# The second MLP matmul as seven half-size products (Strassen's identity) instead of eight, in a fused attention and MLP kernel

## The chip, the cores and the metric

One core of a Trainium2 chip runs the kernel. The time is the device time of one execution in microseconds (us); the kernel before took 689.41 us (median of 3 runs, 689.25 to 690.89). The engines are PE (TensorE, matmuls; PEld is its weight loading), DVE (VectorE), ACT (ScalarE), POOL (GpSimd), and SP, whose queue issues most of the DMAs. Each engine works through its own instructions in program order and waits on semaphores for the others.

## The reference

The input `x` is 2048 tokens by 512. The output mixes two branches by a gate per token:

```python
x = A_x
g = _sigmoid((x * gate_w).sum(-1, keepdims=True))
a = _A_ref(x, A_wqkv, A_wo)                 # 32 heads of 16, causal window of 256, then @ wo
b = _B_ref(x, B_w1, B_b1, B_w2, B_b2)       # gelu(layernorm(x) @ w1 + b1) @ w2 + b2
return g * a + (1 - g) * b
```

The change touches the last product of `_B_ref`, `h @ w2`: `h` is 2048 tokens by 1792 (the hidden width F), `w2` is 1792 by 512. All of it is float32.

## The kernel before, in words

A float32 product is made of three matmuls on `float32r` operands: every operand is split into a high part (a rounded copy, by ACT's `copy` or a DVE cast) and a low part (`lo_part`, line 132: the value minus its high part, a DVE subtraction with two operands in SBUF), and high x high, high x low and low x high are summed in PSUM.

The program runs in stages. Up to about 110 us the projections for q, k and v are made. Up to about 480 us attention runs, with the first MLP matmul (line 651) filled in between; its results, before the activation, go to DRAM as `hp`, a block of 128 hidden rows by 512 tokens for each of 4 token chunks and 14 hidden blocks. The last stage, from 487 us on, is the one that the change rewrites. It is one loop over 56 items (chunk c, hidden block f). For each item PE runs 12 matmuls (line 881, `mlp2`): 4 blocks of 128 tokens by three high/low pairs; the stationary operand is 128x128 of `h`, the moving one is a 128x512 part of `w2`. Four PSUM banks collect a chunk over its 14 items.

What feeds the loop is written out by hand in program order. `load_h` brings a block of `hp` six items ahead, ACT applies the GELU (line 707) two items ahead, DVE makes the high part (cast, line 711) and the low part (line 133) one item ahead. In chunk 0 the blocks of `w2` are split as well (ACT copy, DVE subtraction).

Into the same loop goes the attention's output projection, `attn_out`, once for each chunk and for 4 blocks b of 128 tokens. `scale(b)` multiplies the attention's sum by the reciprocal of its denominator (DVE, line 839) and splits the product (ACT copy, DVE subtraction). `mm(b)` runs 12 matmuls with `wo` (line 850), then ACT scales the result by the gate (line 857) and DVE adds the bias share (line 858; chunk 0 is finished on line 853 instead). `after(n, f)` queues `f` for n items later. The four `scale(b)` are queued when `attn_out` is called, each `mm(b)` when its `scale(b)` runs; so at one item `scale(b + 1)` stands ahead of `mm(b)`. Two PSUM banks (`o0`, `o1`) take the `mm` in turn.

At a chunk's last item, line 895 adds the four MLP sums, times the gate, into the output block `us` and stores it (chunk 0: lines 889 and 890). The functions around the change, in the numbering of the profile:

Of the kernel before, what the change touches and what calls it, by code (L numbers as in the profile page):

```python
# [19 lines left out]
S = 2048  # L20
# [6 lines left out]
FT = F // 128  # L27
C = 512
# [33 lines left out]
def gated_mix_kernel(ctx, tc: tile.TileContext, xt, x2, wq0, wqk, wv, wo, xa, gw, w1, w2, b1, b2, out):  # L62
# [608 lines left out]
    w2s, wos, w2t, spare = {}, {}, [], []  # L671

    def load_w2(f):
        if f % 2 == 0:
            w2t.append(x8())
            if f == 2:
                spare.append(x8())
        w = w2s[f] = w2t[-1][:, f % 2 * 2 * C:f % 2 * 2 * C + 2 * C].rearrange("p (k n) -> p k n", k=2)
        raw = t2()
        sp.dma_start(raw, w2[f])  # L680
        return lambda both=False: split(w, raw, both)
# [7 lines left out]
    def early_w2():  # L689
        for n in range(6):  # L690
            def go(n=n):
                fn = load_w2(n)
                after(2, lambda: fn(True))
            after(1 + n, go)
# [5 lines left out]
    hs = {}  # L700

    def load_h(c, f):
        s = t2()
        sp.dma_start(s, hp[c, f])

        def gelu():
            act.activation(s, s, AF.Gelu_apprx_tanh, bias=b1s[:, f:f + 1])  # L707

        def parts(dst=None):
            h, l = dst or (t2(F32R), t2(F32R))  # L710
            dve.tensor_copy(h, s)  # L711
            lo_part(l, s, h)
            hs[c, f] = h, l

        return gelu, parts
# [10 lines left out]
    def block(p, kb):  # L726
# [10 lines left out]
        if p == 7 and kb == 12:  # L737
            early.extend(load_h(0, f) for f in range(2))
# [39 lines left out]
    for f, (gelu, _) in enumerate(early):  # L778
        gelu()
# [16 lines left out]
    nt[0] = 28  # L796
    waiting = {}
    for f in range(2, 4):
        waiting[0, f] = load_h(0, f)
    for f in range(4, 6):  # L800
        waiting[0, f] = load_h(0, f)
# [3 lines left out]
    for f in range(2, 4):  # L805
        waiting[0, f][0]()
        waiting[0, f] = (lambda: None), waiting[0, f][1]
    low, high = {"o0": 1, "o1": 1, "a4": 1, "a5": 1}, {f"a{i}": 1 for i in range(4)}
    open_psum(*((low, high) if "b0" in used else (high, low)))
    b2s = get("work", "b2s", 1, (128, D))  # L810

    after(1, gate)
    after(4, lambda: early_wo(2, 4))
    after(7, lambda: sp.dma_start(b2s, view(b2, [0, 128], [1, D])))
    us = {}

    def attn_out(c):
# [154 lines left out]
```

## Time and profile before

| | |
|---|---|
| median of 3 runs | 689.41 us |
| the profiled execution, its own time | 689.64 us |
| its span (first to last instruction) | 687.8 us |
| PE busy over the span | 681.1 us (99%) |
| last stage, 487.0 to 683.8 us: PE / DVE / ACT / POOL busy | 196.64 / 108.55 / 62.73 / 0.00 us |
| mean granted TensorE clock | 0.999 |

The span is what the trace covers; 1.8 us of the execution's time lie outside it. Busy times overlap between engines. An instruction's duration includes a run-out that the next one on the same engine may overlap, so that the distance from start to start is shorter than the duration. "128x512" in a row means 128 partitions by 512 elements in each.

### The profile page before, as it was taken

How to read it: one execution, taken by the hardware profiler on the slowest of the kernel's cores; microseconds unless marked ns; L12 is line 12 of the kernel's file. 1: busy time of each engine (PE TensorE's matmuls, PEld its weight loads, DVE VectorE, ACT ScalarE, POOL GpSimd, SP SyncE). 2: the span in 40 equal slices, each digit the busy share in tenths (PEclk: the TensorE clock that was granted, in tenths of full speed). 3: DMA queues.
4: the chain of work that ended last, by engine and by line, in shares of the span. 5: the costliest groups of instructions: out<-in, count | busy, mean ns of one | idle time of the engine just before them, and what ended most of it. 6: DMA issues, size and time to landing. Idle time of an engine off the chain costs nothing.

```text
span 687.8 us, 15593 instructions
## 1 busy us (share of the span) xinstructions
PE 681.1 (99%) x5674; PEld 535.5 (78%) x5674; DVE 476.4 (69%) x970; ACT 384.6 (56%) x637; POOL 265.9 (39%) x622
## 2 busy tenths in 40 slices
PE   9999999999999999999999999999999999999997
PEld 6887777877768777877787777777787888888886
DVE  6737789968777787777686877855575545556454
ACT  6438453457677776877758777687633224123231
POOL 6800156426666664765656566568000000000000
PEclk9999999999999999999999999999999999999999
DMA  8998888786575767566676555527876450841801
GB/s 322 354 290 266 278 262 267 217 253 224 176 211 173 247 211 228 174 214 188 190 240 207 168 185 153 178 96 240 288 238 204 143 173 5 275 126 41 253 1 62
DMA packets 89620, 137.91 MB, mean 200 GB/s; under 512 B 13160, under 2 KB 36648, under 8 KB 89416
## 3 DMA queue, kind: packets, MB, share of 16 engines
q1 hardware_dynamic: 81384, 128.72, 59.1%
q10 hardware_dynamic: 8160, 8.19, 3.9%
q8 instruction: 45, 0.74, 0.4%
q14 instruction: 31, 0.25, 0.1%
HBM read 81.53 MB, written 54.30 MB: 197 GB/s over the span
## 4 chain that ended last, share of the span: by engine, by line
PE 96%; ACT 1%; DVE 1%; DMA 1%; issue 0%; POOL 0%; SPq 0%; DVEq 0%; ACTq 0%
PE ps_b L651 22%; PE ps_a L881 22%; PE ps_b L441 13%; PE ps_d L308 12%; PE ps_b L418 7%; PE ps_b L362 7%; PE ps_d L338 7%; PE ps_o L850 6%; PE ps_d L295 1%; PE ps_x L362 1%; DMA qk<-qk 1%; PE ps_x L279 1%; ACT x L420 0%; DVE us L895 0%; DVE us L889 0%; ACT pb L420 0%
## 5 line engine op out<-in xcount | busy, mean ns | idle before, releaser
L651 PE MATMUL ps_b<-x,w 64*128 64x512 f32 x1344 | 207.1, 393 | 0.0
L881 PE MATMUL ps_a<-x,t 128*128 128x512 f32 x648 | 150.2, 389 | 0.2 <-DVE t L711 0.2
L372 DVE TENSOR_REDUCE mx<-ps_b 128x2 f32<-128x512 f32 x208 | 144.1, 693 | 7.1
L881 PEld LDWEIGHTS ps_a<-x,t 128*128 128x128 f32 x648 | 121.5, 188 | 26.2 <-DVE t L711 0.6
L651 PEld LDWEIGHTS ps_b<-x,w 64*128 64x128 f32 x1344 | 127.4, 186 | 10.5 <-ACT x L136 0.3
L371 DVE COPY_PREDICATED ps_b<-tri,ps_b 128x256 f32<-128x256 uint8 x208 | 88.4, 425 | 52.7 <-PE ps_b L362 40.6
L422 POOL TENSOR_SCALAR_AFFINE_SELECT pa<-pa 128x256 f32<-128x256 f32 x192 | 74.2, 414 | 57.7 <-ACT pa L420 56.7
L420 ACT ACTIVATE pa<-ps_b 128x768 f32<-128x768 f32 x96 | 76.5, 813 | 24.7 <-PE ps_b L418 13.3
L418 PE MATMUL ps_b<-qk 50*128 50x384 f32 (+5 forms) x512 | 87.8, 339 | 0.1
L308 PE MATMUL ps_d<-x,w 128*128 128x512 f32 x360 | 84.7, 390 | 0.0
L362 PE MATMUL ps_b<-qk 62*128 62x384 f32 (+3 forms) x472 | 83.0, 345 | 1.0 <-DMA qk<-qk 0.8
L308 PEld LDWEIGHTS ps_d<-x,w 128*128 128x128 f32 x360 | 67.3, 188 | 14.5 <-issue 0.5
L420 ACT ACTIVATE pb<-ps_b 128x768 f32<-128x768 f32 (+2 forms) x96 | 66.2, 706 | 20.5 <-PE ps_b L418 9.7
L422 POOL TENSOR_SCALAR_AFFINE_SELECT pb<-pb 128x256 f32<-128x256 f32 x160 | 62.2, 415 | 37.4 <-ACT pb L420 36.9
L707 ACT ACTIVATE t<-t,b1s 128x512 f32<-128x512 f32 x56 | 38.6, 716 | 44.0 <-DMA t<-hp 43.6
L418 PEld LDWEIGHTS ps_b<-qk 50*128 50x128 f32 (+1 forms) x512 | 48.8, 184 | 16.0 <-issue 3.2
L422 POOL TENSOR_SCALAR_AFFINE_SELECT x<-x 128x256 f32<-128x256 f32 x128 | 49.3, 414 | 29.7 <-ACT x L420 29.3
L420 ACT ACTIVATE x<-ps_b 128x768 f32<-128x768 f32 x64 | 50.7, 813 | 14.0 <-PE ps_b L418 9.7
L362 PEld LDWEIGHTS ps_b<-qk 62*128 62x128 f32 (+1 forms) x472 | 45.1, 184 | 17.2 <-issue 3.9
L338 PE MATMUL ps_d<-wv,x 128*128 128x512 f32 x192 | 46.7, 394 | 0.0
L850 PE MATMUL ps_o<-w,t 128*128 128x512 f32 x192 | 46.1, 389 | 0.0
L441 PE MATMUL ps_b<-pa,v 128*32 128x128 f32 (+2 forms) x704 | 42.9, 345 | 0.3 <-ACT x L420 0.2
(96 smaller groups left out, 757.1 us busy)
## 6 DMA issues: line engine op xcount, KB each, us to landing
qk<-qk SPq DMA_DIRECT2D x112, 196.0 KB
t<-hp SPq DMA_DIRECT2D x56, 256.0 KB
hp<-t SPq DMA_DIRECT2D x54, 256.0 KB
qk<-t SPq DMA_DIRECT2D x48, 256.0 KB
osc<-x SPq DMA_DIRECT2D x31, 256.0 KB
t<-in_w SPq DMA_DIRECT2D x28, 256.0 KB
w<-w SPq DMA_DIRECT2D x28, 256.0 KB
qk<-t ACTq DMA_DIRECT2D x24, 256.0 KB
```

Of the source, the lines that this page charges most:

```text
L308: pe.matmul(o, a[:, dt * 128:(dt + 1) * 128], b[:, dt * C:(dt + 1) * C], start=n == 0, stop=n == 11)
L338: pe.matmul(o, x[:, a:a + 128], wvs[dt][:, k], start=n == 0, stop=n == 11)
L362: pe.matmul(o[:, e, :n], qs[pr][r:k, qb * 128:qb * 128 + 128], ks[pr][r:k, t0:t0 + n], start=True, stop=True)
L371: dve.copy_predicated(o[:, :, :128], tri, o[:, :, 256:384])
L372: dve.tensor_reduce(m, o[:, :, :256], mybir.AxisListType.X, ALU.max)
L418: pe.matmul(o[:, e, :w], ks[pr][r:k, kb * 128:kb * 128 + 128], qs[pr][r:k, kb * 128:kb * 128 + w], start=True, stop=True)
L420: act.activation(pt[:, :, :w], o[:, :, :w], AF.Exp, scale=0.25)
L422: pool.affine_select(out=pt[:, :, a:a + 128], in_=pt[:, :, a:a + 128], pattern=[[0, 2], [sgn, 128]], base=b, channel_multiplier=-sgn, comp ...
L441: pe.matmul(a[32 * h:32 * h + 32, at:at + w], vs[:, kb, v:v + 32], pts[p, kb][:, h, fr:fr + w], start=n == 0, stop=n == len(parts) - 1, sk ...
L651: pe.matmul(o[:, e], w[kt // 4][r:r + 64, k, m:m + 128], y[r:r + 64, a:a + C], start=n == 0, stop=n == 23)
L850: pe.matmul(a, x[:, g], wos[g][:, k], start=n == 0, stop=n == 11)
L881: pe.matmul(accs[c][b], x[:, b * 128:(b + 1) * 128], w, start=f == 0 and n == 0, stop=f == FT - 1 and n == 2)
```

## The change

Strassen's identity multiplies two 2x2 block matrices with seven block products instead of eight. Here a token chunk is halved (256 + 256 tokens), the hidden axis is halved (block i and block i + 7 go together), and the 512 outputs are halved (256 + 256). One step s is such a pair of hidden blocks in one chunk: 7 steps in each chunk, 28 in all. In each step, `product(s, k)` for k = 0 to 6 runs 6 matmuls (line 1013 of the changed kernel): 2 blocks of 128 tokens by three high/low pairs, now with a 128x256 moving operand. Seven PSUM banks, one for each k, collect a chunk.

The operands of the seven products are sums and differences of the quarters of `h` (5 of them, and 2 quarters as they are) and of `w2` (again 5 and 2). Per step, POOL makes the 5 sums of `h`, and for steps 1 to 6 POOL makes 3 and DVE 2 of the sums of `w2` (`sums`, line 696 by way of `mix`). Each of the 7 operands is then split: ACT copies 256 + 256 + 1280 columns, DVE subtracts the same (line 134). Casts on DVE are gone from this stage. `w2`'s operands are made in chunk 0 and kept. `h` has two sets of operands in turn. Step 0 is prepared in the attention stage.

At the last step of a chunk, `spread(c, k)` adds each product, times plus or minus the gate, into the one or two output quarters that contain it: 24 DVE instructions of 128x256 (line 1021) where there were four of 128x512. In the last chunk the last two steps run interleaved, product by product. `attn_out` is now placed by a table of (step, product) places; `mm` has one PSUM bank.

```diff
+NP = FT // 2
...
+    def part(pair, x, a, b):
+        low, high = (f(a, b) for f in pair)
+        copy(high, x)
+        lo_part(low, x, high)
+
+    def pairs_of(a, b):
+        a, b = (room(t) for t in (a, b))
+        return a(0, 1), a(1, 2), b(0, 1), b(1, 2)
+
+    def mix(to, x, y, op, eng):
+        eng.tensor_tensor(out=to, in0=x, in1=y, op=op)
+
+    def sums_w(raw, ab, ks, eng, n=0):
+        a0, a1, b0, b1 = ab
+        sums = ((a1, b1, ALU.subtract), (a0, b0, ALU.subtract), (a0, a1, ALU.add), (b0, b1, ALU.add), (a0, b1, ALU.add))
+        for k in ks:
+            mix(raw(k - n, k - n + 1), *sums[k], eng)
+
+    def sums_h(raw, ab, ks, eng, n=0):
+        a0, a1, b0, b1 = ab
+        sums = {2: (a1, a0, ALU.subtract), 3: (b1, b0, ALU.subtract), 4: (a0, b1, ALU.add),
+                5: (a0, b0, ALU.add), 6: (a1, b1, ALU.add)}
+        for k in ks:
+            mix(raw(k - n, k - n + 1), *sums[k], eng)
...
-    t = spare[0]
-    rooms = [(t[:, f * 2 * C:f * 2 * C + C], t[:, f * 2 * C + C:f * 2 * C + 2 * C]) for f in range(2)]
-    for f in range(2):
-        early[f][1](rooms[f])
+    hs = {0: [room(x8()[:, :NP * 256]) for _ in range(2)]}
+    ab = pairs_of(*early)
+    part(hs[0], ab[0], 0, 1)
+    part(hs[0], ab[3], 1, 2)
+    for ks in ((2, 3), (4,), (5, 6)):
+        raw = room(t2())
+        sums_h(raw, ab, ks, dve if ks[0] < 5 else pool, ks[0])
+        part(hs[0], raw(0, len(ks)), ks[0], ks[-1] + 1)
...
+    def raw_w(i):
+        tag = (None, "ra", "us0", "us1", "high6", "us1", "us1")[i]
+        t = get("work", tag, 1, *(((128, NP * 256),) if tag == "high6" else ((128, 4, 512),)))
+        if tag != "high6":
+            t = t.rearrange("p a n -> p (a n)")
+        return room(t[:, :5 * 256])
+
+    def sums(kind, s, *engs):
+        ab = pairs_of(*raws[kind, s])
+        raw = wholes[kind, s] = raw_w(s) if kind == "w" else room(get("work", "r", 2, (128, 5 * 256)))
+        if kind == "w":
+            sums_w(raw, ab, (0, 1), engs[0])
+            sums_w(raw, ab, (2, 3, 4), engs[1])
+        else:
+            t = raws[kind, s][0]
+            sums_h(raw, ab, (2, 3, 4, 5, 6), engs[0], 2)
...
+    def parts_h(s):
+        ab, raw = pairs_of(*raws.pop(("h", s))), wholes.pop(("h", s))
+        if s == 1:
+            hs[1] = [seven(f"h{x}") for x in "lh"]
+        hs[s] = hs[s % 2]
+        part(hs[s], ab[0], 0, 1)
+        part(hs[s], ab[3], 1, 2)
+        part(hs[s], raw(0, 5), 2, 7)
+
+    def ahead(s):
+        if s < NPS:
+            gelu(s % NP, raws["h", s])
+        if s < NP:
+            sums("w", s, dve, pool)
+        if s < NPS:
+            sums("h", s, pool)
+
+    def parts(s):
+        if s < NPS:
+            parts_h(s)
+        if s < NP:
+            parts_w(s)
...
-        def scale(b, o, r):
+        def scale(b):
+            o, r = (t[x][:, :, b * 128:b * 128 + 128] for x in "or")
             dve.tensor_tensor(out=o, in0=o, in1=r, op=ALU.mult)
-            h, l = t2(F32R, (128, 4, 128)), t2(F32R, (128, 4, 128))
+            h, l = t[b] = t2(F32R, (128, 4, 128)), t2(F32R, (128, 4, 128))
             copy(h, o)
             lo_part(l, o, h)
 
-            def mm():
-                i = 4 * c + b
-                a = ps(f"o{b % 2}")
-                n = 0
-                for x, k in ((h, 0), (h, 1), (l, 0)):
-                    for g in range(NG):
-                        pe.matmul(a, x[:, g], wos[g][:, k], start=n == 0, stop=n == 11)
-                        n += 1
-                if not c:
-                    dve.scalar_tensor_tensor(out=us[c][:, b], in0=a, scalar=g0[:, i:i + 1], in1=us[c][:, b],
-                                             op0=ALU.mult, op1=ALU.add)
-                    sp.dma_start(out[i], us[c][:, b])
-                    return
-                act.activation(us[c][:, b], a, AF.Copy, scale=g0[:, i:i + 1])
-                dve.scalar_tensor_tensor(out=us[c][:, b], in0=b2s, scalar=g1[:, i:i + 1], in1=us[c][:, b],
+        def mm(b):
+            i = 4 * c + b
+            if not b:
+                us[c] = get("work", f"us{c % 2}", 1, (128, 4, 512))
+            h, l = t.pop(b)
+            a = ps("o")
+            n = 0
+            for x, k in ((h, 0), (h, 1), (l, 0)):
+                for g in range(NG):
+                    pe.matmul(a, x[:, g], wos[g][:, k], start=n == 0, stop=n == 11)
+                    n += 1
+            act.activation(us[c][:, b], a, AF.Copy, scale=g0[:, i:i + 1])
+            dve.scalar_tensor_tensor(out=us[c][:, b], in0=b2s, scalar=g1[:, i:i + 1], in1=us[c][:, b],
+                                     op0=ALU.mult, op1=ALU.add)
+
+        n = NP * c if c else 3
+        at(*((n - 6, 1) if c else (0, 2)), load_su)
+        at(*((n - 5, 1) if c else (0, 6)), inv)
+        at(*((n - 3, 5) if c else (1, 1)), load_o)
+        at(*((n - 2, 1) if c else (1, 5)), load_r)
+        for b, (p, q) in enumerate((((n - 1, 4), (n, 1)), ((n, 1), (n, 4)), ((n, 4), (n + 1, 1)), ((n + 1, 1), (n + 1, 4)))):
+            at(*p, lambda b=b: scale(b))
+            at(*q, lambda b=b: mm(b))
...
+    adds = {0: ((0, 1, 1), (1, 1, 1)), 1: ((0, 0, -1), (1, 0, -1)), 2: ((1, 1, 1),), 3: ((0, 0, -1),),
+            4: ((0, 0, 1), (1, 1, 1)), 5: ((0, 0, -1), (0, 1, 1)), 6: ((1, 0, 1), (1, 1, -1))}
+    accs = {}
+
+    def product(s, k):
+        c, i = divmod(s, NP)
+        if not i:
+            accs[k] = ps(f"a{k}")
+        (hl, hh), (wl, wh) = ([f(k, k + 1) for f in p] for p in (hs[s], w2s[i]))
+        for b in range(2):
+            for n, (x, w) in enumerate(((hh, wh), (hh, wl), (hl, wh))):
+                pe.matmul(accs[k][:, 256 * b:256 * b + 256], x[:, 0, b * 128:(b + 1) * 128], w[:, 0],
+                          start=not i and not b and not n, stop=i == NP - 1 and n == 2, skip_group_check=True)
+
+    def spread(c, k):
+        for row, col, sg in adds[k]:
+            for b in range(2):
+                i = 4 * c + 2 * row + b
+                u = us[c][:, 2 * row + b, col * 256:col * 256 + 256]
+                dve.scalar_tensor_tensor(out=u, in0=accs[k][:, 256 * b:256 * b + 256], scalar=sign[sg][:, i:i + 1], in1=u,
                                          op0=ALU.mult, op1=ALU.add)
...
+    parts(1)
+    for s in range(NPS - 2):
+        c, i = divmod(s, NP)
+        if s:
+            tick()
+            parts(s + 1)
+        ahead(s + 2)
+        if s + 3 < NPS:
+            load_raw("h", s + 3)
+        if s + 3 < NP:
+            load_raw("w", s + 3)
+        for k in range(NP):
+            for fn in plan.pop((s, k), []):
+                fn()
+            product(s, k)
+            if i == NP - 1:
+                spread(c, k)
+        if i == NP - 1:
+            for row in range(2):
+                store(c, row)
+    parts(NPS - 1)
+    c = NCH - 1
+    for k, row, cols in ((0, 0, None), (1, 0, None), (4, 0, None), (5, 0, (256, 512)), (6, 1, (0, 256)),
+                         (2, 1, (256, 512)), (3, 0, (0, 256))):
+        for s in (NPS - 2, NPS - 1):
+            product(s, k)
+        spread(c, k)
+        if cols:
+            store(c, row, slice(*cols))
+    assert not plan
```

Three places show how the instructions move. The first is DVE's queue around the output projection of chunk 1, before. L839 is `scale`'s product, the L133 after it the low part of `scale`, L858 the bias share at the end of `mm`; L711 with its L133 split a block of `h`:

```order
L839 TENSOR_TENSOR oa_7177<-oa_7177,ra_7178 128x4x128
L133 TENSOR_TENSOR t_7494<-oa_7177,t_7493 128x512
L858 SCALAR_TENSOR_TENSOR us_7216<-b2s_6889,g_86,us_7216 128x512
L711 CAST t_7514<-t_7336 128x512
L133 TENSOR_TENSOR t_7515<-t_7336,t_7514 128x512
L839 TENSOR_TENSOR oa_7177<-oa_7177,ra_7178 128x4x128
L133 TENSOR_TENSOR t_7533<-oa_7177,t_7532 128x512
L858 SCALAR_TENSOR_TENSOR us_7216<-b2s_6889,g_86,us_7216 128x512
```

The same queue of the changed kernel, at the output projection of chunk 2. L987 is the bias share, L970 `scale`'s product; the L134 with `hl` or `x_517` are the low parts of the next step's `h`:

```order
L987 SCALAR_TENSOR_TENSOR us_649_8172<-b2s_6917,g_86,us_649_8172 128x512
L970 TENSOR_TENSOR oa_7975<-oa_7975,ra_8015 128x4x128
L134 TENSOR_TENSOR t_8190<-oa_7975,t_8189 128x512
L987 SCALAR_TENSOR_TENSOR us_649_8172<-b2s_6917,g_86,us_649_8172 128x512
L970 TENSOR_TENSOR oa_7975<-oa_7975,ra_8015 128x4x128
L134 TENSOR_TENSOR t_8231<-oa_7975,t_8230 128x512
L134 TENSOR_TENSOR x_517_6824<-g_8070,x_518_6825 128x256 x2
L134 TENSOR_TENSOR x_517_6824<-r_8156,x_518_6825 128x1280
L987 SCALAR_TENSOR_TENSOR us_649_8172<-b2s_6917,g_86,us_649_8172 128x512
L970 TENSOR_TENSOR oa_7975<-oa_7975,ra_8015 128x4x128
L134 TENSOR_TENSOR t_8295<-oa_7975,t_8294 128x512
```

What moved: before, `scale` of the next block (L839) had run ahead of the bias share (L858) of the block whose matmuls were under way; the rows L839, L133, L858 belong to blocks b + 1, b + 1 and b. Now the bias share of block b (L987) stands ahead of `scale(b + 1)` (L970), since `mm(b)` and `scale(b + 1)` have the same place in the table and `mm(b)` was entered first.

The second place is the changed DVE queue at the end of chunk 1 (L1021 is `spread`; the first two rows are the low parts for the step that follows):

```order
L134 TENSOR_TENSOR x_517_6824<-g_7942,x_518_6825 128x256 x2
L134 TENSOR_TENSOR x_517_6824<-r_8000,x_518_6825 128x1280
L1021 SCALAR_TENSOR_TENSOR us_613_7627<-ps_a_612_7620,g_86,us_613_7627 128x256 x4
L1021 SCALAR_TENSOR_TENSOR us_613_7627<-ps_a_617_7648,z,us_613_7627 128x256 x4
L1021 SCALAR_TENSOR_TENSOR us_613_7627<-ps_a_618_7655,g_86,us_613_7627 128x256 x2
L1021 SCALAR_TENSOR_TENSOR us_613_7627<-ps_a_619_7662,z,us_613_7627 128x256 x2
L970 TENSOR_TENSOR oa_7975<-oa_7975,ra_8015 128x4x128
L134 TENSOR_TENSOR t_8111<-oa_7975,t_8110 128x512
L1021 SCALAR_TENSOR_TENSOR us_613_7627<-ps_a_623_7689,g_86,us_613_7627 128x256 x4
```

What moved: `scale(0)` of the next chunk now stands among the 24 `spread` instructions, and the next step's low parts stand ahead of them; before, four additions (L895) took the place of the 24.

The third place is POOL. Before, its last work was the masking of the attention probabilities; the changed queue goes on behind that (`ra`, `us` and `high` are rooms for sums of `w2`, `r` for sums of `h`):

```order
L423 AFFINE_SELECT pb_1524<-pb_1524 128x2x128 x4
L696 TENSOR_TENSOR t_6839<-t_6671,t_6672 128x256 x2
L696 TENSOR_TENSOR ra_6863<-g_6852 128x256 x3
L696 TENSOR_TENSOR r_6869<-g_6849 128x256 x5
L696 TENSOR_TENSOR us_546_6944<-g_6858 128x256 x3
L696 TENSOR_TENSOR r_6950<-g_6855 128x256 x5
```

So POOL, which had nothing in the last stage, has 8 two-operand sums for each step up to step 6 and 5 for each step after it.

More of the change, by code (lines that the diff above doesn't have):

```diff
@@ L698, in early_wo, with load_h, gelu @@
         after(k, lambda: [fn() for fn in fns])
[L700 to L715, printed above, removed]
+    def load_h(c, i, raws):
+        for k in range(2):
+            sp.dma_start(raws[k], hp[c, i + NP * k])
+    def gelu(i, raws):
+        for k in range(2):
+            f = i + NP * k
+            act.activation(raws[k], raws[k], AF.Gelu_apprx_tanh, bias=b1s[:, f:f + 1])
     cur = [None]
@@ L795, in gated_mix_kernel, with load_raw, seven @@
     open_pool("work")
[L796 to L801, printed above, removed]
+    nt[0] = 3
+    raws = {}
+    def load_raw(kind, s):
+        t = get("work", "g", 4, (128, 2, 512))
+        raws[kind, s] = [t[:, k] for k in range(2)]
+        if kind == "w":
+            load_w2(s, raws[kind, s])
+        else:
+            load_h(s // NP, s % NP, raws[kind, s])
+    def seven(tag):
+        return room(get("work", tag, 1, (128, NP * 256), F32R))
```

184 lines of the change are left out of this document (91 added, 93 removed).

## The prediction

> **What bounds the kernel now.** I read the page's busy shares first, then the engines over the last stage, then the groups of that stage.
>
> ```profile
> span 687.8 us, 15593 instructions
> PE 681.1 (99%) x5674; PEld 535.5 (78%) x5674; DVE 476.4 (69%) x970; ACT 384.6 (56%) x637; POOL 265.9 (39%) x622
> 487.00:683.80 196.80, 196.64 (x866) 161.92 (x864) 108.55 (x186) 62.73 (x98) 0.00 (x0) 1.00 0.47 149
> ```
>
> The third row is the stage that the change rewrites (columns: stretch, length, busy time of PE, PEld, DVE, ACT and POOL, granted clock, DMA). PE works 196.64 of its 196.80 us at full clock; POOL does nothing. PE's own instructions set the time here, and DVE and ACT have slack on average.
>
> ```profile
> L881 PE MATMUL ps_a<-x,t 128*128 128x512 f32 x648 | 150.2, 389 | 0.2 <-DVE t L711 0.2
> L850 PE MATMUL ps_o<-w,t 128*128 128x512 f32 x192 | 46.1, 389 | 0.0
> 545.05 2.88 PE L850 MATMUL ps_o<-w,t 128*128 128x512 f32 x12
> 547.77 2.88 PE L881 MATMUL ps_a<-x,t 128*128 128x512 f32 x12
> ```
>
> From the timeline's starts, 12 matmuls take 547.77 - 545.05 = 2.72 us: 0.227 each from start to start (389 ns is pipelined duration).
>
> **What the change saves on PE.** 28 steps of 42 matmuls with 256 columns replace 28 x 24 with 512. The trace has few of 256:
>
> ```profile
> 357.61 0.28 PE L418 MATMUL ps_b<-qk 64*128 64x256 f32 x2
> 357.73 0.40 PE L651 MATMUL ps_b<-x,w 64*128 64x512 f32 x2
> L881 PEld LDWEIGHTS ps_a<-x,t 128*128 128x128 f32 x648 | 121.5, 188 | 26.2 <-DVE t L711 0.6 <-DVE t L133 0.4
> ```
>
> After a 256-wide pair the next pair starts 0.12 us later, with new weights in both row halves. The other end is the 188 ns that a weight load lasts, if it did not overlap. I take 0.120, since that row has the very width. A step then costs 42 x 0.120 = 5.04 us on PE (a product 0.72) against 24 x 0.227 = 5.44: 28 x 0.40 = 11.2 us saved, not an eighth, because every matmul carries some 13 ns beside its columns (0.227 for 512, 0.120 for 256: the line through both leaves 0.013). The Trainium skill, TensorE: Matmul & The Clock Gate, section Back-to-back issue gap, puts a matmul at N / 2.4 + 2.5 ns; by it the step would fall from 5.2 to 4.6 us and the saving be 16 us. The trace's 227 ns against its 216 speaks for my figure.
>
> **What it adds, and its prices.**
>
> ```profile
> 9.72 4.30 DVE L133 TENSOR_TENSOR x<-v,x 128x512 fp32r<-128x512 f32 x7
> L133 DVE TENSOR_TENSOR t<-oa,t 128x512 fp32r<-128x512 f32 x16 | 11.1, 693 | 12.0 <-ACT t L136 12.0
> L858 DVE SCALAR_TENSOR_TENSOR us<-b2s,g,us 128x512 f32<-128x512 f32 x12 | 9.0, 752 | 28.1 <-ACT us L857 28.1
> L895 DVE SCALAR_TENSOR_TENSOR us<-ps_a,g,us 128x512 f32<-128x512 f32 x11 | 7.7, 751 | 3.3 <-PE ps_a L881 3.3
> L895 DVE SCALAR_TENSOR_TENSOR us<-ps_a,g,us 128x256 f32<-128x256 f32 x2 | 0.9, 480 | 0.0
> L707 ACT ACTIVATE t<-t,b1s 128x512 f32<-128x512 f32 x56 | 38.6, 716 | 44.0 <-DMA t<-hp 43.6
> L136 ACT ACTIVATE w<-wv 128x128 fp32r<-128x128 f32 x8 | 2.2, 300 | 2.4 <-DMA wv<-in_wq 2.4
> L136 ACT ACTIVATE t<-oa 128x512 fp32r<-128x512 f32 x16 | 10.1, 632 | 45.9 <-DVE oa L839 29.9 <-PE ps_a L881 10.9 <-DMA t<-hp 3.9
> L857 ACT ACTIVATE us<-ps_o,g 128x512 f32<-128x512 f32 x12 | 8.3, 690 | 29.9 <-PE ps_o L850 29.9
> L133 POOL TENSOR_TENSOR w<-t,w 128x512 fp32r<-128x512 f32 x12 | 15.5, 1292 | 5.8 <-ACT w L136 5.7
> L133 POOL TENSOR_TENSOR nm<-mx,nm 128x16 fp32r<-128x16 f32 x32 | 7.1, 222 | 2.7
> L422 POOL TENSOR_SCALAR_AFFINE_SELECT pa<-pa 128x256 f32<-128x256 f32 x192 | 74.2, 414 | 57.7 <-ACT pa L420 56.7
> ```
>
> DVE: seven subtractions in 4.30 us are 0.60 apart, 0.09 less than one lasts. The two L895 rows give 1.06 ns a column, so a two-operand instruction of 256 columns takes 0.33, of 1280 columns 1.41. The low parts of one step's `h` cost 0.33 + 0.33 + 1.41 = 2.07 us; `w2`'s as much, plus two sums, 0.66. A `spread` instruction is 0.39 (480 ns less 0.09), 24 of them 9.4 us. ACT: from 300 and 632 ns, 0.41 for 256 columns, 1.30 for 1280; a step with both splits and two GELUs is 5.7 us at full durations. POOL: no 256-wide sum is in the trace. Its ends are the one-operand 414 ns and the 512-wide 1292; the line through 222 (16 columns) and 1292 gives 0.74, 0.65 apart, and I take that, since work and operands are the same. An estimate from the Trainium skill's floor of 2.5 cycles an element at 1.2 GHz (GPSIMD Engine Reference, section 2.1) is 0.53 us; by it the result would be some 9 us lower, and the 512-wide row, 1292 against 1067, stands above it.
>
> **The shared port.** DVE and POOL do not run such work side by side:
>
> ```profile
> 100.94 0.65 DVE L133 TENSOR_TENSOR t<-ps_d,t 128x512 fp32r<-128x512 f32 x1
> 101.51 1.07 DVE L133 TENSOR_TENSOR x<-t,x 128x512 fp32r<-128x512 f32 x1
> 100.74 1.29 POOL L531 TENSOR_TENSOR t<-t,t 128x512 f32<-128x512 f32 x1
> 119.61 2.89 DVE L133 TENSOR_TENSOR x<-t,x 128x512 fp32r<-128x512 f32 x2
> 118.74 3.20 POOL L531 TENSOR_TENSOR t<-t,gws 128x512 f32<-128x512 f32 x2 [0.81 <-DMA t<-in_x]
> ```
>
> POOL's sum from 100.74 ends at 102.03. The DVE subtraction that reads PSUM runs through it in 0.65; the next, with both operands in SBUF, ends at 102.58, 0.55 after POOL. At 119 both engines pay for each other. So in the changed stage POOL's sums and DVE's low parts, `scale` and bias instructions share one resource; `spread`, which reads PSUM, does not.
>
> **Chunk 0.** A step of 1 to 6 holds that port for 8 x 0.65 (POOL) + 2.07 + 2.07 + 0.66 (DVE) = 10.0 us, twice PE's 5.04. Step 1 is prepared while PE runs step 0: begun with the stage, its pieces need 10.0 plus the last ACT copy (1.30) and DVE's 1.41, so PE waits about 12.7 - 5.0 = 7.7. Steps 1 and 2: 10.0 plus about 1 us in which the port idles while ACT copies between POOL's fifth sum and DVE's subtraction, less 5.04: 2 x 6 = 12. Steps 3 to 6 must make three more such sets (33), step 7's `h` (5 x 0.65 + 2.07 + 1 = 6.3), and four blocks of the projection with three 0.6 us instructions (7.2): 46.5 against PE's 4 x 5.04 + 4 x 2.72 = 31.0, so 15.5. Together 35 us.
>
> **The projection's order.** `mm(b)` now precedes `scale(b + 1)`. From the end of `mm(b)` to the start of `mm(b + 1)` stand PE's run-out 0.16 (389 - 227 ns), ACT 0.69, bias 0.75, product 0.69, copy 0.63, low part 0.69: 3.6 us in a row, where before the first part lay under the next `scale`. PE has three or four products in between, 2.16 or 2.88 us.
>
> **Each chunk change** (into chunks 1, 2, 3). DVE's queue from the last step's start: low parts 2.07, 24 `spread` 9.4, `scale(0)` 1.9 (0.60 + 0.63 + 0.69), the next step's low parts 2.07, bias 0.66, `scale(1)` 1.9: 18.0 us before `mm(1)`. PE has 5.04 + 0.72 + 2.72 + 2.16 = 10.6: late by 7.4. `mm(2)`: 3.6 - 2.88 = 0.7. `mm(3)`: 3.6 + 2.07 (low parts behind it) - 2.16 = 3.5. That is 11.6, plus port waits of 12 such DVE instructions, 0 to 0.65 each: 3.9 in the middle. 15.5 x 3 = 46.5 us. Behind a waiting DVE low part stand the next `spread` and `scale`; behind the waiting `mm` all later products.
>
> **The end and the clock.** Steps 26 and 27 interleave, so 27's pieces are wanted six products (4.3 us) earlier; the last `spread` adds about 1. The clock: PE has no idle gap in this stage before, but some nine of over 3 us after. At the kernel's start it shows what a cold array costs:
>
> ```profile
> 1.25 4.45 PE L279 MATMUL ps_x<-t 128*128 128x512 bf16 x10 [1.25 <-DVE t L275]
> 686.00:687.80 1.80, 0.00 (x0) 0.00 (x0) 0.00 (x0) 0.00 (x0) 0.00 (x0) 0.53 0.19 64
> ```
>
> Ten matmuls take 4.45 us where 2.27 would do, 2.2 lost, and the granted clock falls to 0.53 within four idle us at the end. Ends: 0 (the slow matmuls run while DVE is the bound) to 9 x 2.2 = 20; I take 7, one in each chunk change. The Trainium skill (TensorE: Matmul & The Clock Gate, HAM oscillation) has the clock halve after a gap of about 3.4 us, which agrees with the 0.53.
>
> **Sum.** 687.8 - 11.2 + 35 + 46.5 + 5.3 + 7 = 770.4 us of span; the profiled execution lay 1.8 above its span (689.64; the median of the runs is 689.41), so 772.
>
> **Rivals.** *The port costs nothing* (sums quick, or spread over idle moments). Chunk 0 is then bound by ACT, about 0.5 a step over PE: 3, the first step 5, its projection chains 8; chunk changes 3 x 11.6 = 35; end 5.3: 687.8 - 11.2 + 56 + 1.8 = 735 to 745. For it: on average DVE has room (108.55 of 196.8 us). Against: the two port rows. *All hidden, faster*: steps are prepared two ahead; if the prepared pieces always arrive and each chain fits under 2.16 us, only PE counts: 687.8 - 11.2 + 1 + 1.8 = 679. It decides from the point where 3.6 becomes less than 2.16, and a chunk-0 step less than 5.04; POOL's empty 196.8 us speaks for it, every price above against. *Weight loads bind* at 0.188: a step is 7.9 us, 69 more on PE, which hides part of the waits (chunk 0 12, changes 27, end 5): 687.8 + 69 + 44 + 1.8 = 803. The 0.12 row speaks against it.
>
> **Chances.** My sum 0.60 (its own range 752 to 795), port free 0.25, all hidden 0.06, weight loads 0.05, something between all hidden and port free 0.04. The range 735 to 803 leaves out the hidden cases and the tails. A difference of 0.3% (2 us) is about what runs of this kernel can tell: faster 0.07, same 0.01, slower 0.92.
>
> **What would show it.** L1013 starts 0.120 apart within a product; PE idle for 80 us or more in the stage, waiting for L134 (DVE low parts), most of it in steps 1 to 9 and behind L984 after each chunk change, and little in steps 3 to 5 of later chunks; POOL's L696 at 0.74 or more each, the 1280-wide L134 above 1.5 on the mean; the granted clock below 1 there. I am wrong if PE is busy throughout, or if the 256-wide matmuls are 0.19 apart.

## The result: 13% slower, and the profile after

The changed kernel takes 780.88 us (median of 4 runs, 779.29 to 781.02) against 689.33 us for the kernel before on the same chip: a ratio of 1.132, 95% interval 1.129 to 1.135. The prediction was 772 us with a range of 735 to 803, so direction and size were right and the sum was 9 us short. The page of the changed kernel, in the same order as before (span, busy shares, PE's 40 slices, the granted clock in the same slices, the chain that ended last):

```profile
span 778.4 us, 17049 instructions
...
PE 701.5 (90%) x6178; PEld 570.6 (73%) x6178; DVE 551.1 (71%) x1048; ACT 443.0 (57%) x739; POOL 407.8 (52%) x777
...
PE   8999999999999999999999999655768985995795
...
PEclk9999999999999999999999999886798997998999
...
PE 69%; DVE 12%; ACT 5%; DMA 5%; issue 4%; POOL 4%; SPq 1%; ACTq 0%; DVEq 0%; POOLq 0%
```

PE was 96% of the chain before and is 69% now. Nothing happens to the first 25 slices. The last 15 are the stage that was rewritten: a long dent at its start (chunk 0 and the change to chunk 1), then two short ones at the next two chunk changes. The windows view, cut at the first product of steps 0, 7, 14 and 21 (columns: stretch, length, busy PE, PEld, DVE, ACT, POOL, granted clock, DMA share, GB/s):

```profile
489.00:579.30 90.30, 59.92 (x344) 54.27 (x342) 67.62 (x82) 42.43 (x71) 55.31 (x56) 0.81 0.44 141
579.30:645.50 66.20, 52.75 (x342) 48.23 (x343) 39.58 (x59) 26.84 (x43) 31.13 (x36) 0.90 0.33 106
645.50:710.10 64.60, 52.71 (x342) 48.33 (x343) 39.50 (x59) 26.84 (x43) 31.06 (x36) 0.89 0.33 109
710.10:772.90 62.80, 51.72 (x342) 47.13 (x342) 40.46 (x68) 22.50 (x36) 23.95 (x28) 0.92 0.15 51
772.90:778.40 5.50, 0.00 (x0) 0.00 (x0) 2.78 (x8) 0.00 (x0) 0.00 (x0) 0.73 0.55 191
```

At full speed a chunk needs 7 x 5.04 + 4 x 2.72 = 46.2 us of PE. So chunk 0 is 44.1 us late, the others 20.0, 18.4 and 16.6. The stage lasts 283.9 us where four times 46.2 is 184.8: 99.1 us of lateness, which turn the 12 us that PE was to save (196.8 to 184.8) into 87.1 lost. The span's other 3.5 us are a stage that begins 2.0 us later and a tail 1.5 us longer.

The lateness has two kinds. From start to start of neighbouring matmuls in this stage, 24 intervals of over 0.7 us sum to 73.6 us (PE waits), and 168 intervals of 1.3 to 2.6 times the usual distance lose another 24.5 us (PE works at about half clock). A group of 12 matmuls, 2.88 us as a row of the kernel before, shows the second kind in the first row below; the second row shows the price of a 256-wide matmul when nothing is late. Both are rows of the chain of the changed kernel:

```profile
593.61 4.61 PE ps_o L984 x12
...
612.57 23.05 PE ps_a L1013 x192
```

23.05 / 192 = 0.120 us, the price that the prediction took. Who waits for whom (the waits view over the stage; total us, times, longest):

```profile
ACT t L137 <- DVE oa L970: 59.5, 16, 10.0
...
PE ps_o L984 <- ACT t L137: 35.7, 12, 4.6
...
PE ps_a L1013 <- DVE us L1021: 12.2, 3, 4.6
PE ps_a L1013 <- DVE x L134: 8.6, 3, 5.0
```

PE's largest entry is the attention projection (line 984), which waits for ACT's copy of its scaled operand; ACT in turn waits for DVE's scaling (line 970). Waits of a product for a DVE low part (line 134) are 13.3 us: 8.6 in the row shown, 2.6 and 2.1 in rows with other operand names. The groups that were disputed (busy us, mean ns of one):

```profile
L696 POOL TENSOR_TENSOR r<-g 128x256 f32<-128x256 f32 x135 | 124.3, 952 | 113.1 <-ACT g L752 113.1
...
L134 DVE TENSOR_TENSOR x<-g,x 128x256 fp32r<-128x256 f32 x32 | 22.6, 745 | 0.2
...
L134 DVE TENSOR_TENSOR x<-us,x 128x1280 fp32r<-128x1280 f32 x2 | 4.0, 2006 | 0.0
```

A sum on POOL lasts 0.95 us, not 0.74. A 256-wide low part on DVE lasts 0.745 us here; the same operation lasts 0.42 where POOL leaves it alone (first experiment). The 1280-wide low parts are stretched only in part: the two in the row and two more, all of chunk 0, take 2.0 us; the other 28 of the stage take 1.51 on the mean, against 1.48 to 1.49 in the run without POOL (`x5_dve`).

### The profile page after: what moved, and what is told of

Same layout as the page of the kernel before. It is cut to its first block, busy times and chain, and to the rows that moved or that the text cites. A ratio compares the mean times of both kernels' runs of the same rounds, so it can differ in the third digit from the quotient of the medians.

```text
span 778.4 us, 17049 instructions
## 1 busy us (share of the span) xinstructions
PE 701.5 (90%) x6178; PEld 570.6 (73%) x6178; DVE 551.1 (71%) x1048; ACT 443.0 (57%) x739; POOL 407.8 (52%) x777
## 4 chain that ended last, share of the span: by engine, by line
PE 69%; DVE 12%; ACT 5%; DMA 5%; issue 4%; POOL 4%; SPq 1%; ACTq 0%; DVEq 0%; POOLq 0%
PE ps_b L652 19%; PE ps_b L442 11%; PE ps_d L309 9%; PE ps_a L1013 7%; PE ps_b L419 6%; PE ps_b L363 6%; PE ps_o L984 5%; PE ps_d L339 4%; DVE us L1021 4%; POOL r L696 4%; DVE x L134 2%; DVE oa L970 1%; DMA qk<-qk 1%; DVE hl L134 1%; ACT t L137 1%
## 5 line engine op out<-in xcount | busy, mean ns | idle before, releaser
L696 POOL TENSOR_TENSOR r<-g 128x256 f32<-128x256 f32 x135 | 124.3, 952 | 113.1 <-ACT g L752 113.1
L652 PEld LDWEIGHTS ps_b<-x,w 64*128 64x128 f32 x1344 | 127.5, 186 | 10.5 <-ACT x L137 0.3
L984 PE MATMUL ps_o<-w,t 128*128 128x512 f32 x192 | 66.3, 512 | 35.7 <-ACT t L137 35.7
L421 ACT ACTIVATE pa<-ps_b 128x768 f32<-128x768 f32 x96 | 76.5, 812 | 24.7 <-PE ps_b L419 13.3
L984 PEld LDWEIGHTS ps_o<-w,t 128*128 128x128 f32 x192 | 47.4, 255 | 50.0 <-ACT t L137 38.9
L421 ACT ACTIVATE pb<-ps_b 128x768 f32<-128x768 f32 (+2 forms) x96 | 66.3, 707 | 20.2 <-PE ps_b L419 10.8
L1013 PE MATMUL ps_a<-x,x 128*128 128x256 f32 x336 | 45.1, 293 | 10.2 <-DVE us L1021 4.6
L1013 PE MATMUL ps_a<-x,hh 128*128 128x256 f32 x224 | 42.5, 290 | 12.6 <-DVE us L1021 7.6
L1013 PEld LDWEIGHTS ps_a<-x,x 128*128 128x128 f32 x336 | 43.7, 201 | 11.6 <-issue 5.1
```

The lines of the kernel that those rows point to most:

```text
L421: act.activation(pt[:, :, :w], o[:, :, :w], AF.Exp, scale=0.25)
L652: pe.matmul(o[:, e], w[kt // 4][r:r + 64, k, m:m + 128], y[r:r + 64, a:a + C], start=n == 0, stop=n == 23)
L696: eng.tensor_tensor(out=to, in0=x, in1=y, op=op)
L984: pe.matmul(a, x[:, g], wos[g][:, k], start=n == 0, stop=n == 11)
L1013: pe.matmul(accs[k][:, 256 * b:256 * b + 256], x[:, 0, b * 128:(b + 1) * 128], w[:, 0], start=not i and not b and not n, stop=i == NP - 1 ...
```

## The experiments

Twelve kernels were run, each beside runs of the kernel before, and ratios are against those. Diffs are against the changed kernel.

**The port, and POOL's slowness.** `x4_port` lets POOL read and add only 8 of the 256 columns and fills the rest with a constant, so the sums are not Strassen's.

```diff
     def mix(to, x, y, op, eng):
+        if eng is pool:
+            eng.tensor_tensor(out=to[:, :, :8], in0=x[:, :, :8], in1=y[:, :, :8], op=op)
+            eng.memset(to[:, :, 8:], 0.25)
+            return
```

> Each of POOL's sums of 256 columns sums only 8 columns and fills the other 248 with a constant: POOL keeps its instructions, its waits and about its time (0.25 for the small sum and 0.33 for the fill against 0.74), but hardly reads SBUF; the output is not the reference's. Port theory (sums and DVE's two-operand instructions exclude one another): DVE's 256-wide low parts fall from 0.73 back to 0.42 us, the time to 735 to 755. Rival (no exclusion, POOL is just slow and late): DVE's durations as now, time 770 or more, since POOL's own time per step falls by less than 1.5 us and it idles half of the stage.

Measured: 743.9 us, ratio 1.078 (1.075 to 1.080). Groups, and the windows of chunks 0 and 1, of this kernel:

```profile
L697 POOL TENSOR_TENSOR r<-g 128x8 f32<-128x8 f32 x135 | 49.6, 368 | 125.7 <-ACT g L756 125.7
...
L134 DVE TENSOR_TENSOR x<-g,x 128x256 fp32r<-128x256 f32 x32 | 12.0, 416 | 0.2
```

```profile
489.50:567.60 78.10, 56.61 (x344) 51.35 (x343) 48.13 (x82) 41.94 (x71) 35.13 (x116) 0.83 0.50 160
567.60:623.30 55.70, 50.07 (x343) 46.64 (x344) 34.15 (x60) 26.84 (x43) 19.67 (x71) 0.94 0.37 126
```

37 us go, 12.2 of them in chunk 0 and 10.5, 6.8 and 6.0 in the others. The DVE low part of the very same shape falls from 745 to 416 ns although nothing was done to DVE. The run does not separate the shared resource from POOL's own shorter work: a sum with its fill is 0.67 us here instead of 0.95.

**All sums on DVE.** `x5_dve` takes POOL out altogether, at the price of DVE's time.

```diff
-            sums("w", s, dve, pool)
+            sums("w", s, dve, dve)
...
-            sums("h", s, pool)
+            sums("h", s, dve)
```

> All 256-column sums of hidden and weight blocks on VectorE instead of GpSimd (135 sums move), nothing else. Theory (a sum on GpSimd holds the shared port and stretches VectorE's low parts from 0.42 to 0.73 us, and is slow itself): a sum costs VectorE about 0.33 us instead of 0.95 on GpSimd, the late operands of chunk 0 come earlier, 753 to 765 us, that is 15 to 28 less than the change; the 256-wide low parts fall under 0.5 us. Rival (VectorE, busy 71% of the span already, becomes the queue that all wait in): 778 us or more.

Measured: 765.63 us (764.74 to 766.34), ratio 1.109 (1.105 to 1.113): 15 us less, 0.6 us beyond the weak edge of the theory's range and far from its rival's. The group of the sums on DVE, and the window of chunk 0:

```profile
L696 DVE TENSOR_TENSOR r<-g 128x256 f32<-128x256 f32 x135 | 47.5, 418 | 0.0
```

```profile
488.30:575.60 87.30, 57.11 (x344) 51.52 (x343) 66.75 (x140) 42.34 (x71) 0.00 (x0) 0.84 0.44 142
```

In chunk 0, DVE now does 58 more instructions (x140 against x82) and its busy time does not rise: 66.75 us against 67.62. So POOL's sums had stretched DVE's own instructions by about as much as the sums cost DVE. That is what sharing means here, and the low parts agree (414 ns). The Trainium skill, SBUF — State Buffer, section Who interferes with whom, says that a DVE instruction with two SBUF inputs contends with a GpSimd instruction that reads SBUF; the runs agree, with 745 against 414 to 416 ns. But chunk 0 gains only 3.0 us: the sums still stand in a queue, now DVE's.

**Chunk 0: the weights.** `x6_now` uses the weight operands of step 0 in all steps; weight blocks 1 to 6 are not loaded, summed or split.

```diff
-            sums("w", s, dve, pool)
+            pass
...
-            parts_w(s)
+            w2s[s] = w2s[0]
```

> The second layer's weights are not prepared: the block of step 0 is used for all steps of chunk 0 and after (no loads, sums or splits of weight blocks 1 to 6); the hidden blocks' sums and splits stay. Theory (chunk 0 is late because both operand sets are prepared in it): 20 to 26 us of the 44 that chunk 0 is late go, 753 to 762 us, with step 7 at 62 to 68 us after step 0 instead of 90. Rival (chunk 0 is late by the attention projection and its loads, or by the hidden blocks alone): 770 to 781 us, step 7 at 80 us or more.

Measured: 758.48 us, ratio 1.099 (1.092 to 1.105). Chunk 0 cut at step 3, the first step with projection blocks (windows): from there to step 7 in the changed kernel; both parts in this one; and the second part in `x1_floor`, below:

```profile
518.80:579.30 60.50, 39.67 (x218) 34.95 (x216) 41.82 (x51) 23.55 (x40) 28.92 (x29) 0.80 0.39 122
```

```profile
488.60:507.90 19.30, 17.09 (x128) 16.78 (x127) 13.45 (x20) 11.81 (x21) 12.01 (x14) 0.91 0.47 154
507.90:558.50 50.60, 34.22 (x218) 30.80 (x217) 24.78 (x32) 20.00 (x31) 22.13 (x25) 0.87 0.39 125
```

```profile
504.80:545.50 40.70, 34.14 (x219) 30.85 (x218) 13.33 (x24) 5.28 (x8) 0.00 (x0) 0.92 0.20 72
```

Step 7 comes 69.9 us after step 0 instead of 90.3: the weights are 20.4 of the 44.1 us, about half of that before step 3 (29.8 to 19.3) and half behind it (60.5 to 50.6). The expectation's 62 to 68 was 2 us too early.

**No operands at all.** `x1_floor` uses both operands of step 0 in every step: nothing is loaded, summed or split for the products after that. What is left is PE's work, the projection and `spread`.

```diff
     def parts(s):
+        hs[s], w2s[s % NP] = hs[0], w2s[0]
+        return
```

(and an early `return` in the functions that load and activate.)

> All steps use the operands prepared for step 0: the loads, GELUs, sums and splits of the other steps are left out, so the output is not the reference's; the 1176 matmuls, the 96 spread instructions and the attention projection stay as they are. My theory (PE's own sum is 11 us smaller, the rest of the 91 us is lost in preparing operands and in the order of the projection): chunk 0 loses only its projection chain, each chunk change the 24 spreads and three waits of about 1 to 1.5 us, so 690 to 710 us, middle 704. Rival A (256-wide matmuls are slow as such, by weight loads or by the cold array): still above 740. Rival B (only the preparation costs, the order of the projection and the spreads are hidden): 679 to 682.

Measured: 708.18 us, ratio 1.027 (1.024 to 1.029). The preparation of operands is 73 of the 92 us between the kernels. And without any of it the new stage is still slower than the old one: PE's 12 us are more than lost again in the projection and the chunk changes. Chunk 0 is 10.9 us late here (57.1 against 46.2), so its 44.1 split into 20.4 of weights, 10.9 that stay without any operand work (9.7 of them in steps 3 to 6, which hold the projection), and a remainder of 12.8 for the hidden blocks. The split is in this order of leaving out; no run leaves out the hidden blocks alone.

**The order of projection and scaling.** `x3_swap` (in the full kernel) and `x2_floor_swap` (with `x1_floor`'s operands) place `scale(b + 1)` ahead of `mm(b)`, as before the change.

```diff
             at(*p, lambda b=b: scale(b))
+        for b, q in enumerate(((n, 1), (n, 4), (n + 1, 1), (n + 1, 4))):
             at(*q, lambda b=b: mm(b))
```

> The full change, only scale(b + 1) ahead of mm(b). My theory: the serial chain goes, but DVE's backlog and the shared port stay: 10 to 18 us less than 781, so 763 to 771. Rival (the port and the preparation decide everything, the projection's order is covered by them): 777 to 782.

> As the kernel with step 0's operands throughout (same work left out), and scale(b + 1) stands ahead of mm(b) again. My theory (a chain of 3.6 us against 2.16 or 2.88 us of products at each of the three changes from block to block, four chunks): 11 to 15 us less than with the changed order, so 688 to 694 us. Rival (the waits at the chunk change come from the 24 spreads alone, the order does not matter): within 3 us of the run without the swap.

Measured: 767.38 us in the full kernel, ratio 1.112 (1.110 to 1.115), as expected: 13.5 us less, and the gaps of 2.05 us ahead of the fourth block in chunks 1 to 3 are gone. With free operands 702.94 us, ratio 1.019 (1.016 to 1.022): a miss, 5.2 us under `x1_floor` and 9 above the forecast. Two gaps remain at every chunk change, of 1.4 and 2.4 us. DVE in that kernel, from the last products of chunk 0 on (timeline):

```profile
547.09 1.65 DVE L1026 SCALAR_TENSOR_TENSOR us<-ps_a,g,us 128x256 f32<-128x256 f32 x4
...
549.44 1.65 DVE L1026 SCALAR_TENSOR_TENSOR us<-ps_a,g,us 128x256 f32<-128x256 f32 x4
551.01 0.87 DVE L1026 SCALAR_TENSOR_TENSOR us<-ps_a,z,us 128x256 f32<-128x256 f32 x2
551.79 0.68 DVE L974 TENSOR_TENSOR oa<-oa,ra 128x512 f32<-128x512 f32 x1
```

`scale(1)` (here line 974) stands behind all 24 `spread` instructions whatever its order against `mm(0)`. That the spreading is what the projection waits for was a reading of this row; the next runs test it.

**The projection away from the chunk change.** `x7_shift_swap` moves the whole projection of chunks 1 to 3, its loads too, three steps later; `x11_late_swap` moves only scaling and matmuls and leaves the loads; `x12_floor_late` is the latter with free operands.

```diff
-        n = NP * c if c else 3
+        n = NP * c + 3 if c else 3
```

```diff
         at(*((n - 2, 1) if c else (1, 5)), load_r)
+        n = n + 3 if c else n
```

> As the exchange of scale and projection blocks, and the projections of chunks 1 to 3 start three steps later in their chunk. Theory (a chunk change is late because the spreading out of seven products, the first splits of the new chunk and the projection's scaling are all queued on VectorE in the same two steps): 747 to 757 us, 10 to 20 less than the exchange alone, and the gaps of PE ahead of L984 in chunks 1 to 3 shrink. Rival (the delay is of TensorE's PSUM banks and ScalarE's evacuation, and moves along with the projection): 763 to 769 us, as the exchange alone.

> As the shifted projection, but only scaling and projection of chunks 1 to 3 move three steps later; their loads stay where the change has them. Theory (the shift lost its gain to its loads: the chain there ran over oa from osc, 7.9 us, and a further load, 9.4 us, since they queue with the hidden loads): the 9 to 11 us gaps ahead of the first projection block go and the time is 740 to 757 us. Rival (a projection in mid-chunk costs as much in waits as at the chunk's start): 765 us or more.

> Operands of step 0 used in every step (no hidden or weight block after step 0 is loaded, summed or split), scale and projection exchanged, and those of chunks 1 to 3 three steps later. Theory (with operands free, what is left at a chunk change is the 24 spreading sums, 0.39 us apart on VectorE, queued ahead of the projection's scaling): 689 to 697 us, 6 to 14 less than with the exchange alone (702.9), gaps of 1.4 and 2.4 us gone. Rival (the banks that the spreading frees late cost TensorE the same): 700 to 704 us.

`x7_shift_swap`: 773.39 us, ratio 1.121 (1.116 to 1.125), 6 us worse than the exchange alone and outside both expectations. Its chain of waits in chunk 1 names why:

```profile
590.89 7.87 DMA oa<-osc
598.77 9.38 DMA g<-hp
...
608.27 0.70 DVE oa L970
...
609.68 4.40 PE ps_o L984 x12
```

The attention sums and denominators are asked for among hidden blocks of the same queue, and DVE's scaling starts 17 us after that (the view puts the second wait down to a hidden block's load; the scaling itself reads only `oa` and `ra`), so PE stands for 9 to 11 us and then runs at half clock: 4.40 us for 12. With the loads left early, `x11_late_swap` takes 751.25 us, ratio 1.091 (1.087 to 1.094), as expected: 16 us under the exchange alone. Chunks 1 to 3 are then 8.7, 9.7 and 9.9 us late instead of 16.0, 14.4 and 15.8 with the exchange alone. Chunk 1 of `x11_late_swap`, and chunks 0 and 1 of `x12_floor_late`:

```profile
575.90:630.80 54.90, 49.04 (x343) 45.79 (x343) 39.99 (x59) 26.96 (x43) 32.41 (x36) 0.97 0.37 124
```

```profile
488.60:544.10 55.50, 48.37 (x344) 45.59 (x343) 18.55 (x36) 9.13 (x15) 0.00 (x0) 0.94 0.29 99
544.10:591.60 47.50, 46.81 (x344) 44.44 (x344) 18.62 (x38) 5.30 (x8) 0.00 (x0) 1.00 0.19 70
```

`x12_floor_late` takes 692.8 us, ratio 1.0053 (1.0038 to 1.0068), in the range of the theory. Its chunk changes cost 1.3 us each: 47.5 against 46.2. So with free operands and the projection out of the way, banks that `spread` frees late cost PE almost nothing (gaps of 0.87 us). And this kernel, whose operands cost nothing, is still half a per cent slower than the one before: chunk 0 alone gives back 9.3 of the 12 us, 8.0 of them in the steps that hold its projection, whose first block waits 6.2 us.

**Chunk 0's loads.** On the chain of the changed kernel the first projection block of chunk 0 hangs on two loads:

```profile
514.65 6.96 DMA oa<-osc
521.63 7.08 DMA ra<-rd
...
528.83 0.70 DVE oa L970
```

`x9_early` asks for both a step earlier; `x14_late0_dve` instead puts that projection one step later, on top of `x13_late_dve` (next).

```diff
-        at(*((n - 3, 5) if c else (1, 1)), load_o)
-        at(*((n - 2, 1) if c else (1, 5)), load_r)
+        at(*((n - 3, 5) if c else (0, 2)), load_o)
+        at(*((n - 2, 1) if c else (0, 6)), load_r)
```

> Chunk 0's attention sums and inverse denominators are asked for one step earlier (the first with the denominators in step 0, the second right behind the reciprocal), nothing else. Theory (the chain of the change runs 14 us over these two loads, oa from osc and ra from rd, each 7 us, which are issued late behind the hidden loads): the first projection block comes 5 to 10 us earlier and the time is 771 to 777 us. Rival (VectorE is late by as much with the splits of steps 1 to 3, so the loads' lateness is covered): 779 to 782 us, no change.

Measured: 783.04 us, ratio 1.135 (1.129 to 1.140): no gain. Its chain has other loads in their place:

```profile
507.30 8.35 DMA t<-in_wo
...
520.69 8.94 DMA g<-in_w
```

Loads that were overtaken, of the projection's and the MLP's weights, are late now: moving one load ahead made others late.

**Gains together.** `x13_late_dve` is `x11_late_swap` with all sums on DVE.

> The late projection of chunks 1 to 3, the exchange, and all 256-column sums on VectorE together. Theory (the gains are of different waits and add: about 13 of the exchange, 15 of the sums, 10 to 25 of the late projection): 728 to 750 us, below every single edit, still over the kernel before. Rival (they share one queue, VectorE, so that the sums moved there take back what the late projection frees): 755 us or more.

> As the kernel with the late projection and the sums on VectorE, and chunk 0's scaling and projection one step later too. Theory (in chunk 0 the first projection block waits 5 to 8 us for its loads; one step later they have landed): 3 to 8 us less than that kernel. Rival (VectorE and ScalarE are late with operands by then whatever the place): within 2 us of it.

Measured: 751.45 us (750.17 to 752.93), ratio 1.090 (1.087 to 1.092), no different from `x11_late_swap` without the sums moved. It reached neither expectation's range, but the gains did not add. Chunks 0 and 1:

```profile
488.30:574.60 86.30, 58.28 (x345) 52.38 (x343) 66.78 (x140) 44.62 (x75) 0.00 (x0) 0.82 0.44 143
574.60:632.80 58.20, 52.01 (x343) 48.24 (x343) 45.04 (x94) 26.51 (x43) 0.00 (x0) 0.91 0.36 116
```

Chunk 1 is 3.3 us longer than in `x11_late_swap`, chunk 0 0.9 shorter. Part of the two gains is one and the same wait: the last step of chunks 1 and 2 lasts 10.8 us with the exchange alone, and 6.2 to 6.3 us in `x5_dve`, in `x11_late_swap` and here, so some 9 us could be won only once. The 15 us that `x5_dve` gained and the 16 of the late projection also come out of the same queue, DVE's, which the projection's scaling shares with everything else: DVE does 5 us more work in chunk 1 than in `x11_late_swap` (45.04 against 39.99). That this takes back the rest is a reading; no run tests it. `x14_late0_dve` measured 751.03 us, ratio 1.090 (1.088 to 1.091), its rival's case: one step later helps nothing.

No version that computes the whole result comes near the kernel before. The best, at 751 us, are 4% under the change and 9% over the old kernel.

## Why the prediction was right, and where its sum was off

**PE's saving: right.** 0.120 us a matmul gave 11.2 us; the stage's need at full speed went from 196.8 to 184.8, by 12.0. (The other saving named there, 16 us, is 17 by the two step times beside it.) The rival in which weight loads bind at 0.188 falls with the row of 192 matmuls in 23.05 us.

**Chunk 0: 35 predicted, 44.1 measured.** The terms for steps 0 to 2 were too large: step 3 was to start 34.8 us after step 0 (3 x 5.04 + 7.7 + 12) and started 29.8 us after. The term for steps 3 to 6, "46.5 against PE's" 31.0, is the one that failed: they took 60.5. It counted work on the shared port and left out that the projection's two loads hold 14 us of the chain, that its blocks wait in turn on DVE and ACT (a block's scaling queues behind the splits of the next step), and that PE then works at a granted clock of 0.80. Of the 29.5 us by which these steps are late, 22.4 are waits and 6.7 slow matmuls. With free operands the same steps still take 40.7.

**Chunk changes: 46.5 + 4.3 + 7 = 57.8 predicted for steps 7 to 27, 55.0 measured.** The queue named there is on the chain: DVE's `spread`, low parts and scaling. The chain of the changed kernel between the last products of chunk 0 and the second projection block, in the prediction's order:

```profile
585.04 4.00 DVE us L1021 x10
...
589.81 1.81 DVE x L134 x2
591.62 0.66 DVE us L987
592.29 0.62 DVE oa L970
...
592.92 0.64 ACT t L137
```

`x11_late_swap` and `x12_floor_late`, which take the projection out of this queue, show that it waited there. The terms are not where they were put. `mm(1)` was to be 7.4 us late; at the change into chunk 1 the waiting is spread over a product that waits 3.3 us for its bank, `mm(0)` (3.6 us, counted as nothing) and `mm(1)` (3.2). At the other two changes the wait for the bank is 4.9 us. `mm(3)` was to be 3.5 late and was 2.05 late; the exchange took that away.

The wait for the bank has a cause that the prediction put at nothing. It started DVE's queue at the last step's first product, as if the sums lay ready. But the operands of `h` go round a loop: POOL's five sums, ACT's copy of them, then ACT's GELU of a later step, which stands behind that copy in ACT's queue and which POOL's next sums wait for. Where nothing else holds it up the loop takes 6.57 us a step (POOL starts at 745.74, 752.31 and 758.88) against PE's 5.04, and by the last step of a chunk PE has caught up with it. The chain there, end of chunk 1:

```profile
635.62 0.72 ACT g L752
...
636.40 0.89 POOL r L696
637.79 3.19 POOL r L696 x4
641.01 1.28 ACT x L137
642.31 1.49 DVE x L134
643.80 1.24 DVE us L1021 x4
```

Only behind that low part does `spread` free the first bank, and PE stands from 640.9 to 645.5: the last step of chunks 1 and 2 takes 10.8 us. In `x4_port`, where a sum is shorter, it takes 5.04, and in `x5_dve` 6.27. So the forecast for the chunk changes named the right queue, left out this loop, and came close in its total partly by luck.

**The shared port: right in kind, its price measured only in part.** 3.9 us a chunk change were predicted for port waits. DVE's busy time in chunk 1 is 5.4 us longer than in `x4_port` (39.58 against 34.15), and `x4_port` took 10.5, 6.8 and 6.0 us out of the chunks 1 to 3. But 5.8 of it, in chunk 1 and again in chunk 2, is the wait behind the loop above, which hangs on how long POOL's own sums take; so how much of the gain is the port is not shown. The sum on POOL, priced at 0.74 us, lasts 0.95, four of them 0.80 apart (3.19 us in the chain above), against 0.65 in the sum. The rival in which the port costs nothing was put at 735 to 745 us, and `x4_port`, where POOL's sums are nearly taken off it, gives 743.9.

**The clock: 7 predicted, 24.5 us of PE's time measured.** The prediction took one cold start of 2.2 us in each chunk change. There are more: of the 15 gaps of 2.98 us or more, 13 are followed by matmuls at about half rate before the next gap. In steps 7 to 27 the slow matmuls lost 13.8 us, twice the 7, while the waits there sum to 40.2 us against the 50.8 of the forecast's other two terms (46.5 + 4.3). The two errors offset each other, which is luck. How much of the slowness is on the path that sets the end was not tried by itself; a filler that keeps PE warm would have to stand in PE's own queue and delay the work.

**All hidden, 679 us: refuted.** The preparation does not fit under PE's 5.04 us a step in chunk 0, and `x12_floor_late` shows that even free operands leave 692.8.

**What was to be seen.** Steps 3 to 5 of chunks 1 to 3 run at 5.04 us each, as said. PE's idle time was to be 80 us or more; it is 73.6, since part of the loss is slow work. It was to wait "for L134"; 13.3 us are that, and most of the rest is a wait for the projection's operand, a few instructions further down the same DVE queue. The 1280-wide low parts were to be above 1.5 us on the mean and are at 1.57; without the four in chunk 0 it is 1.51, hardly more than without POOL.

The sum, then: 770.4 us of span were forecast and 778.4 measured, 8.0 short: 9.1 in chunk 0, -2.8 in the chunk changes, -0.8 in PE's need, and 2.5 at the stage's start and tail.

## What to carry to other kernels

A scheme that saves matmuls by adding elementwise sums has to be priced on the engines that make the sums, with their queues in program order: here PE could win 12 us at most, and the kernel became 92 us slower, because DVE, POOL and ACT could not do that work in time. Averages hide this, since DVE is busy 71% and POOL 52%; cut the stage at its chunk boundaries, add up each engine's queue there, and add up each loop in which engines wait for one another: one of 6.57 us a step held back products of 5.04. Before moving work, look at what its loads pass in their queue: the same projection three steps later was worth 16 us with its loads left early, and cost 6 with the loads moved along.

## What the runs showed of the hardware

- DVE and POOL, both with operands in SBUF, did not add up to two engines: moving 58 sums of chunk 0 from POOL to DVE left DVE's busy time where it was (67.62 and 66.75 us), and a 256-wide low part lasts 0.745 us beside POOL's sums and 0.414 where POOL does nothing (`x5_dve`).
- Two kinds of gap ahead of a projection block of 12 matmuls, at the chunk changes of `x2_floor_swap` (timeline, PE: the second block of chunk 1, then that of chunk 2):

```profile
553.82 3.04 PE L988 MATMUL ps_o<-w,t 128*128 128x512 f32 x12 [2.12 <-ACT us L990]
```

```profile
603.94 4.59 PE L988 MATMUL ps_o<-w,t 128*128 128x512 f32 x12 [2.14 <-ACT us L990]
```

Idle for 2.12 and for 2.14 us, and the same 12 matmuls take 3.04 us after the one and 4.59 after the other. In the traces looked at this way (the change, `x1_floor`, `x2_floor_swap`, `x12_floor_late`) gaps from start to start of up to 1.5 us hardly ever slowed what came next, gaps of 2.0 to 2.6 did in 5 of 10 cases, and those above 3.1 in 14 of 16. The Trainium skill, TensorE: Matmul & The Clock Gate, section HAM oscillation, warns of idle gaps above about 3.4 us; these rows show that shorter ones can cost as much. The same page describes the activity window as free-running; that fits one and the same gap going either way, but that the gap's place in such a window decides was not tried.
